# First layer's sums by a plain copy, factor and bias on GpSimd, a tanh put off near a group's end, and a scale in a register

## The chip, the cores and the metric

The kernel runs on one core of one Trainium2 chip. The metric is the device time of one execution in microseconds. A profile is one further execution, taken by the hardware profiler; its times are those of that execution alone.

A core has five engines that work side by side, each in the order of its own instruction stream: PE (TensorE, matrix products, which read SBUF and write PSUM), DVE (VectorE), ACT (ScalarE, functions of single elements), POOL (GpSimd) and SP (SyncE, which here only issues DMAs). An instruction that needs another engine's result waits for a semaphore, and what stands behind it on its engine waits too.

## The reference

One transformer layer with both branches beside each other, for 2048 rows of 512 columns: a layer norm, then attention with 32 heads of 16, and a dense network with 1792 hidden columns and GELU. Both results are added to the input. Cut to what is computed:

```python
xn = _layernorm(x, axis=-1)
# A: attention
qkv = (xn @ wqkv).reshape(B, S, 3, H, Dh).transpose(2, 0, 3, 1, 4)
scores = jnp.einsum("bhqd,bhkd->bhqk", q, k) * (Dh ** -0.5)
o = jnp.einsum("bhqk,bhkd->bhqd", _softmax(scores, axis=-1), v)
a = o.transpose(0, 2, 1, 3).reshape(B, S, D) @ wo
# B: dense network
h = jax.nn.gelu(xn @ w1 + b1, approximate=True)
b = h @ w2 + b2
return x + a + b
```

All inputs and outputs are float32.

## The kernel before

**Attention sets the beat.** Heads are taken four at a time, 8 groups, and queries 512 at a time, so there are 32 tiles (t), and each has 16 units of 128 rows. A unit (function unit) makes for one step of the schedule four score products S (128 queries by 512 keys, s_half), whose row maximum DVE takes at L259 (mt); four transposed score products T (128 keys by 512 queries, e_half), which ACT turns into exp at L304 (pe); and the products V of such exps with the values (v_half). S runs 20 units ahead of T (LEAD). Every product on PE is written as four matmuls of 32 columns each (tiled, L169), and a head's product uses half of PE's rows.

**The dense work is laid between.** In each unit PE also gets a few products D of the work that is not attention (function dense, a class Group for a sum of such products in one PSUM bank): with the pace MEAN, 3 or 4 products on each half of the rows in a unit. From about 318 to 1430 us of the profile the groups are those of the dense network, made by the function mlp. A **hidden group** makes 128 hidden columns for 512 rows: 12 products on each half, so four units. A **sum group** makes 128 rows of the second layer out of 7 hidden columns' tiles: 21 products on each half, so six units. There are 56 hidden groups and 32 sum groups.

**What follows a group.** When the last product of a group is written, the group's finish is called at once (end), and then the unit's clock goes on by one (tick). For a hidden group this is the function hidden: ACT reads the bank at L1005, multiplies by a factor and adds the bias, each a column with one value per partition, into the tile hh in SBUF. One unit later gelu starts on GpSimd: the square (L983), a scalar step (L984) and a product (L985) make the argument in the tile t (t1 in the code); then ACT takes the tanh at L972, and GpSimd makes from it and hh the two half-precision tiles g (L977 to L980), which the sum groups read as weights of their products. For a sum group the finish is store: ACT reads the bank at L1031 with the factor gs, one column too, into yt, and GpSimd adds it to the tile xa.

**Order.** The order on every engine is that in which the Python code emits. later(n, fn) calls a function n units later. pooled puts steps for GpSimd in a list with an estimate in ns for each; in every unit run_steps takes steps until 2500 ns are used up. The tanh was asked for two units behind the emission of L985, which in a row of hidden groups falls on the unit in which the next hidden group ends.

**Banks.** PSUM has eight banks. S uses three, V one, and T and D share four: T goes round three of them, and D holds one for the length of a group (hold). When a group ends, its bank goes to the end of T's round and the new group takes T's oldest. So the second T product behind a group's end is the last that finds a bank at rest; the third takes the bank that the eviction hh or yt has to empty, and the fourth the bank that the first exp behind the eviction empties.

The scale of the exps is held in a register of ACT (scale_reg), loaded once for every two groups of heads by reg_load (a TENSOR_LOAD in the trace).

Of the kernel before, what the change touches and what calls it, by code (L numbers as in the profile page):

```python
# [10 lines left out]
I32 = mybir.dt.int32  # L11
AF = mybir.ActivationFunctionType
ALU = mybir.AluOpType
# [34 lines left out]
def layer_kernel(ctx: ExitStack, tc: tile.TileContext, x, wqkv, wo, w1, b1, w2, b2, out):  # L48
    nc = tc.nc
# [45 lines left out]
    sexp = const.tile([P, 4], F32, name="sexp")  # L95
# [11 lines left out]
    def banks(tag):  # L107
        k = free_banks[tag].pop(0)
        free_banks[tag].append(k)
        return bank_tile(k, tag)  # L110
# [48 lines left out]
    def given(engine, ns):  # L159
        backlog[engine] += ns  # L160
# [37 lines left out]
            product(user, dst[j:j + 32], lhs[:, j:j + 32], rhs, start=start, stop=stop)  # L198


    scale_reg, held = nc.scalar.alloc_register("exp_scale"), [None]

    def exp_scale(m):

        if held[0] != m:
            nc.scalar.reg_load(scale_reg, sexp[0:1, m:m + 1].bitcast(I32))
            held[0] = m
        return scale_reg

    mt_of, ptiles, pv_of = {}, {}, {}  # L210
    queue, slot = [], [0]
# [1 line left out]
    def later(n, fn, local=False):  # L213
        queue.append((slot[0] + n, fn, local))
# [10 lines left out]
    def pooled(*todo):  # L225
        steps.extend(todo)
# [66 lines left out]
    def e_half(u, n):  # L293

        p, a = divmod(n, 2)
        t, kt = divmod(u, 16)
        g, qb = divmod(t, NQB)
        st = banks("T")
        r = slice(64 * a, 64 * a + 64)
        k0 = (kt % 4) * P  # L300
        tiled(None, st, kst[g % 2][p][kt // 4][r, k0:k0 + P], qst[g % 2][p][qb][r, :], True, True)
        pe = work.tile([P, QB], F32, name="pe", bufs=12)
        ptiles[u, n] = pe
        nc.scalar.activation(pe, st, AF.Exp, scale=exp_scale(g // 2))  # L304
        given("act", 470)

    def v_half(u, a):
# [234 lines left out]
    pos, spent, cur = [0], [False], [None]  # L542
# [103 lines left out]
    with ExitStack() as st1:  # L646
# [245 lines left out]
        gs = const.tile([P, 4], F32, name="gs")  # L892
# [69 lines left out]
    def mlp():  # L962
        m2 = st2p
        w2_s = m2.tile([P, 2, NF, D], F16, name="w2_s")
        b2_b = m2.tile([P, D], F32, name="b2_b")
        done = set()

        def gelu(hh, g, b, f):
            t1 = m2.tile([P, QB], F32, name="t1", bufs=2)

            def tanh():
                nc.scalar.activation(t1, t1, AF.Tanh, scale=GELU_C * GELU_A)  # L972
                given("act", 600)
                later(1, rest, True)

            def rest():
                pooled((690, lambda: nc.gpsimd.tensor_scalar(t1, t1, 1.0, gs[:, 1:2], op0=ALU.add, op1=ALU.mult)),  # L977
                       (1280, lambda: nc.gpsimd.tensor_tensor(t1, t1, hh, op=ALU.mult)),  # L978
                       (620, lambda: nc.gpsimd.tensor_scalar(g[:, 0, f, :], t1, 1.0, 0.0, op0=ALU.mult, op1=ALU.add)),
                       (1160, lambda: nc.gpsimd.tensor_tensor(g[:, 1, f, :], t1, g[:, 0, f, :], op=ALU.subtract)),  # L980
                       (0, lambda: done.add((b, f))))

            pooled((1040, lambda: nc.gpsimd.tensor_tensor(t1, hh, hh, op=ALU.mult)),  # L983
                   (620, lambda: nc.gpsimd.tensor_scalar(t1, t1, 1.0, 1.0 / GELU_A, op0=ALU.mult, op1=ALU.add)),  # L984
                   (1280, lambda: nc.gpsimd.tensor_tensor(t1, t1, hh, op=ALU.mult)),  # L985
                   (0, lambda: later(2, tanh, True)))


        HF = NF // 2
        gts, xas = {}, {}  # L990
        for k in range(NF):
            later(3 * k + 2, lambda k=k: nc.sync.dma_start(w2_s[:, :, k], w2_d[:, :, k]))
        later(12, lambda: nc.sync.dma_start(b2_b, b2[None, :].to_broadcast([P, D])))

        def hidden_group(s, f):
            b, k = s // 2, s % 2 * HF + f
            if f == 0:
                gts[s] = m2.tile([P, 2, HF, QB], F16, name="g", bufs=2)
            g, xb, wc = gts[s], xbs[b], wcs[b * NF + k]
            later(1, lambda: fetch_w1(b * NF + k + 2))  # L1000

            def hidden(hp):
                hh = m2.tile([P, QB], F32, name="hh", bufs=3)
                scale, bias = fac1[0][:, k // 2:k // 2 + 1], b1_s[:, k:k + 1]
                nc.scalar.activation(hh, hp, AF.Identity, bias=bias, scale=scale)  # L1005
                given("act", 700)
                later(1, lambda: gelu(hh, g, s, f), True)

            return Group([lambda c=c, i=i, j=j: (wc[:, i, c, :], xb[:, j, c, :]) for c in range(NC) for i, j in PAIRS],
                         dbank, hidden, pace=MEAN)  # L1010

        def sum_group(s, q):
            b, t, g = s // 2, s // 2 * 4 + q, gts[s]
            if s % 2 == 0:
                xas[t] = m2.tile([P, D], F32, name="xa", bufs=4)
                nc.sync.dma_start(xas[t], x[t * P:(t + 1) * P, :])
                later(3, lambda: pooled((1280, lambda: nc.gpsimd.tensor_tensor(xas[t], xas[t], b2_b, op=ALU.add))), True)
            xa = xas[t]
            if q == 3 and s % 2 == 0:
                fetch_x(b + 1)  # L1020
            if s == 2 * NQB - 1 and q == 1:

                ocs[2] = feed[0].tile([P, 2, NC, QB], F16, name="xb", bufs=1)
                when((NG - 2) * NQB + 2, lambda: read_o(ocs[2], 2, True), 2)
                for k in range(3):
                    acs[8 + k] = feed[0].tile([P, D], F32, name="ac", tag="wc", bufs=3)
                    later(3 + k, lambda k=k: read_acc(acs[8 + k], 8 + k))

            def store(yp):
                yt = m2.tile([P, D], F32, name="yt", bufs=2)  # L1030
                nc.scalar.activation(yt, yp, AF.Copy, scale=gs[:, 2:3])  # L1031
                given("act", 600)
                add = lambda: nc.gpsimd.tensor_tensor(xa, xa, yt, op=ALU.add)  # L1033
                put = lambda: nc.sync.dma_start(acc_d[t * P:(t + 1) * P, :], xa)
                later(1, lambda: pooled((1280, add), (0, lambda: later(4, put, True) if s % 2 else None)), True)

            return Group([lambda f=f, i=i, j=j: (g[:, i, f, q * P:(q + 1) * P], w2_s[:, j, s % 2 * HF + f, :])
                          for f in range(HF) for i, j in PAIRS], dbank, store, lambda n: (s, n // 3) in done, pace=MEAN)

        for f in range(HF):  # L1040
            yield hidden_group(0, f)
        for s in range(1, 2 * NQB + 1):
            for q in range(4):
                yield sum_group(s - 1, q)
                if s < 2 * NQB and q < 3:
                    for f in range(*((0, 3), (3, 5), (5, 7))[q]):
                        yield hidden_group(s, f)
# [143 lines left out]
```

## Time and profile before

| | |
|---|---|
| median of 3 runs | 1552.85 us (1550.26 to 1552.85) |
| the profiled execution | 1555.34 us, of which the span from the first to the last instruction is 1553.6 |
| PE busy | 1514.5 us, 97% |
| DVE busy | 1401.0 us, 90% |
| ACT busy | 1251.6 us, 81% |
| POOL busy | 674.6 us, 43% |
| mean granted PE clock | 0.993 |

Busy time is the union of an engine's instructions. PE's matmuls are pipelined and their ends are modelled, so a PE that looks busy can still be one that waits within its stream. A line such as "418.62 1.09 ACT L304 ACTIVATE pe<-pT ... x2 [0.24 <-PE pS L169]" is a row of the timeline: start and length in us, engine, source line, operation, tile written and tiles read, shapes, how many instructions are merged in the row, and in brackets how long the engine had been idle before and what ended that. In a row of groups the two numbers behind the bar are the busy time and the mean length of one in ns, and behind the second bar stands the idle time just before.

### The profile page before, as it was taken

Reading aid. Unit: us, or ns where it says so; the run is one execution under the profiler, and the core shown is the slowest. Engines: PE = TensorE matmul, PEld = TensorE weight load, DVE = VectorE, ACT = ScalarE, POOL = GpSimd, SP = SyncE. Lnnn points to the kernel's source line nnn. Section 1 sums busy time; section 2 is a strip of 40 time slices with the busy share of each in tenths; the row PEclk is TensorE's granted clock in tenths of the full one; section 3 lists DMA queues with packets and bytes.
Section 4 is the critical chain, followed back from the end, with each engine's and each line's share of the span. In section 5 each row is a group of like instructions: output and inputs, shape, how many; then the busy total and the mean of one; then the engine's idle time right before and its main releaser. Section 6 shows DMA issues by size and latency. Waiting matters only on the chain.

```text
span 1553.6 us, 86338 instructions
## 1 busy us (share of the span) xinstructions
PE 1514.5 (97%) x39203; PEld 806.0 (52%) x39203; DVE 1401.0 (90%) x2372; ACT 1251.6 (81%) x2326; POOL 674.6 (43%) x694
## 2 busy tenths in 40 slices
PE   8998999999999999999999999999999999999997
PEld 4434545555555555555555555555555555555443
DVE  7898989999999999999999999999999999999612
ACT  4316878889888888888888888888888888888771
POOL 3113697546465444435443443555254454521000
PEclk9999999999999999999999999999999999999997
DMA  6454576542111311121112111121112111022412
GB/s 210 124 158 142 167 231 197 180 120 88 50 35 47 91 33 34 36 75 42 35 56 65 46 35 35 35 80 55 36 42 60 45 35 35 22 66 60 150 50 86
DMA packets 113671, 123.72 MB, mean 80 GB/s; under 512 B 24988, under 2 KB 85276, under 8 KB 113304
## 3 DMA queue, kind: packets, MB, share of 16 engines
q1 hardware_dynamic: 113304, 118.21, 25.4%
q8 instruction: 306, 5.01, 1.4%
q14 instruction: 61, 0.50, 0.1%
HBM read 80.61 MB, written 37.34 MB: 76 GB/s over the span
## 4 chain that ended last, share of the span: by engine, by line
PE 84%; DVE 8%; ACT 2%; issue 2%; DMA 2%; SPq 1%; POOL 0%; ACTq 0%; POOLq 0%
PE pV L169 25%; PE pS L169 19%; PE pD L169 19%; PE pT L169 17%; DVE mt L259 6%; PE pT L439 1%; PE pS L439 1%; ACT pe L304 1%; ACT t L972 1%; DVE amx L667 1%; PE pT L532 1%; PE pD L439 1%; DMA ac<-acc_d 0%; PE pV L532 0%; SPq L1064 0%
## 5 line engine op out<-in xcount | busy, mean ns | idle before, releaser
L259 DVE TENSOR_REDUCE mt<-pS 128x1 f32<-128x512 f32 x2048 | 1299.9, 684 | 60.7 <-PE pS L169 43.1
L304 ACT ACTIVATE pe<-pT 128x512 f32<-128x512 f32 x2048 | 1100.0, 598 | 169.5 <-PE pS L169 72.3
L169 PE MATMUL pV<-pe,vv 64*32 64x512 f32 x8192 | 1077.6, 595 | 0.2
L169 PE MATMUL pT<-qst,kst 64*32 64x512 f16 x8192 | 708.2, 378 | 10.4 <-ACT pe L304 8.9
L169 PE MATMUL pS<-kst,qst 62*32 62x512 f16 x8192 | 636.8, 378 | 9.3 <-DVE mt L259 6.0
L169 PEld LDWEIGHTS <-qst 62*32 62x32 f16 x8192 | 271.1, 92 | 226.8 <-issue 77.9
L169 PEld LDWEIGHTS <-kst 64*32 64x32 f16 x8192 | 270.2, 91 | 213.7 <-issue 109.5
L169 PE MATMUL pD<-xb,wc 64*32 64x512 f16 x5376 | 370.5, 377 | 0.0
L169 PE MATMUL pD<-w_s,g 64*32 64x512 f16 x5376 | 359.4, 377 | 0.0
L169 PEld LDWEIGHTS pV<-pe,vv 64*32 64x32 f32 x8192 | 181.5, 105 | 111.2 <-PE pV L169 18.0
L983 POOL TENSOR_TENSOR t<-hh 128x512 f32<-128x512 f32 x56 | 58.3, 1042 | 341.2 <-ACT hh L1005 341.2
L169 PEld LDWEIGHTS <-g 64*32 64x32 f16 x5376 | 113.8, 92 | 38.6
L169 PE MATMUL pD<-xt,wqk_h 64*32 64x512 f16 x1920 | 127.6, 377 | 3.5 <-issue 3.5
L169 PEld LDWEIGHTS <-wc 64*32 64x32 f16 x5376 | 112.6, 91 | 31.1
L360 POOL TENSOR_TENSOR osb<-osb,rb 128x512 f32<-128x512 f32 x31 | 39.9, 1287 | 128.1 <-DMA rb<-den_d 95.1
L1033 POOL TENSOR_TENSOR xa<-xa,yt 128x512 f32<-128x512 f32 x32 | 41.0, 1280 | 119.0 <-ACT yt L1031 119.0
L1070 DVE SCALAR_TENSOR_TENSOR ac<-pS,gs,ac 128x512 f32<-128x512 f32 x20 | 15.0, 751 | 67.0 <-PE pT L169 46.9
L978 POOL TENSOR_TENSOR t<-t,hh 128x512 f32<-128x512 f32 x56 | 71.8, 1283 | 4.7
L985 POOL TENSOR_TENSOR t<-t,hh 128x512 f32<-128x512 f32 x56 | 71.7, 1280 | 4.7
L980 POOL TENSOR_TENSOR g<-t,g 128x512 f16<-128x512 f32 x56 | 65.3, 1166 | 4.7
L977 POOL TENSOR_SCALAR t<-t,gs 128x512 f32<-128x512 f32 x56 | 38.8, 693 | 55.5 <-ACT t L972 55.5
L169 PE MATMUL pS<-wo_s,oc 64*32 64x512 f16 x1008 | 61.7, 378 | 0.3
(139 smaller groups left out, 881.1 us busy)
## 6 DMA issues: line engine op xcount, KB each, us to landing
wch<-in_B_w_dram SPq DMA_DIRECT2D x28, 512.0 KB
wc<-w_d SPq DMA_DIRECT2D x56, 256.0 KB
qk_d<-stg SPq DMA_DIRECT2D x32, 256.0 KB
rb<-den_d SPq DMA_DIRECT2D x124, 64.0 KB
w_d<-wsp SPq DMA_DIRECT2D x28, 256.0 KB
kst<-qk_d SPq DMA_DIRECT2D x128, 48.0 KB
qst<-qk_d SPq DMA_DIRECT2D x128, 48.0 KB
xs<-in_A_x_dram SPq DMA_DIRECT2D x16, 256.0 KB
```

Source lines behind the costliest of these rows:

```text
L169: p = nc.tensor.matmul(*args, **kw)
L259: nc.vector.reduce_max(mt_of[t][:, n, qt, kb:kb + 1], s, axis=AX.X)
L304: nc.scalar.activation(pe, st, AF.Exp, scale=exp_scale(g // 2))
L360: pooled((1280, lambda: nc.gpsimd.tensor_tensor(osb, osb, rb, op=ALU.mult)), (620, lambda: nc.gpsimd.tensor_scalar(ot[:, 0], osb, 1.0, 0.0 ...
L439: nc.tensor.matmul(self.bank, lhs, rhs, start=start, stop=self.last and self.over())
L532: nc.tensor.matmul(pj, xt[:, i, c, t * P:(t + 1) * P], wh[j][:, c, :], start=(n == 0), stop=(n == 11))
L977: pooled((690, lambda: nc.gpsimd.tensor_scalar(t1, t1, 1.0, gs[:, 1:2], op0=ALU.add, op1=ALU.mult)), (1280, lambda: nc.gpsimd.tensor_tenso ...
L978: (1280, lambda: nc.gpsimd.tensor_tensor(t1, t1, hh, op=ALU.mult)),
L980: (1160, lambda: nc.gpsimd.tensor_tensor(g[:, 1, f, :], t1, g[:, 0, f, :], op=ALU.subtract)),
L983: pooled((1040, lambda: nc.gpsimd.tensor_tensor(t1, hh, hh, op=ALU.mult)), (620, lambda: nc.gpsimd.tensor_scalar(t1, t1, 1.0, 1.0 / GELU_A ...
L985: (1280, lambda: nc.gpsimd.tensor_tensor(t1, t1, hh, op=ALU.mult)),
L1033: add = lambda: nc.gpsimd.tensor_tensor(xa, xa, yt, op=ALU.add)
```

## The change

Three edits, all of them on what follows a group.

1. hidden reads the bank by a plain copy, with no factor and no bias. Both are applied by a new GpSimd instruction on hh in place, one unit later, ahead of gelu; gelu itself is called when that step has been emitted.
2. tanh asks, when its time has come, how many products the current group has left. If there is no current group (one has just ended) or no more than 8 are left on both halves together, it comes back one unit later, and is then emitted in any case.
3. store's scale is read from a register of ACT. The code for the exp's register is made general (factor takes the register and the place it is loaded from, and loads it only if it changes).

```diff
-    scale_reg, held = nc.scalar.alloc_register("exp_scale"), [None]
-
-    def exp_scale(m):
-
-        if held[0] != m:
-            nc.scalar.reg_load(scale_reg, sexp[0:1, m:m + 1].bitcast(I32))
-            held[0] = m
-        return scale_reg
+    exp_scale, sum_scale = (nc.scalar.alloc_register(n) for n in ("exp_scale", "sum_scale"))
+    held = {}
+
+    def factor(reg, src):
+
+        if held.get(reg.name) != str(src):
+            nc.scalar.reg_load(reg, src.bitcast(I32))
+            held[reg.name] = str(src)
+        return reg
...
-        nc.scalar.activation(pe, st, AF.Exp, scale=exp_scale(g // 2))
+        nc.scalar.activation(pe, st, AF.Exp, scale=factor(exp_scale, sexp[0:1, g // 2:g // 2 + 1]))
...
-            def tanh():
+            def tanh(again=1):
+                if again and (cur[0] is None or cur[0].left(0) + cur[0].left(1) <= 8):
+                    later(1, lambda: tanh(0), True)
+                    return
                 nc.scalar.activation(t1, t1, AF.Tanh, scale=GELU_C * GELU_A)
...
-                nc.scalar.activation(hh, hp, AF.Identity, bias=bias, scale=scale)
-                given("act", 700)
-                later(1, lambda: gelu(hh, g, s, f), True)
+                nc.scalar.activation(hh, hp, AF.Copy)
+                given("act", 600)
+                later(1, lambda: pooled((690, lambda: nc.gpsimd.tensor_scalar(hh, hh, scale, bias, op0=ALU.mult, op1=ALU.add)),
+                                        (0, lambda: gelu(hh, g, s, f))), True)
...
-                nc.scalar.activation(yt, yp, AF.Copy, scale=gs[:, 2:3])
+                nc.scalar.activation(yt, yp, AF.Copy, scale=factor(sum_scale, gs[0:1, 2:3]))
```

What this does to the order: PE's and DVE's streams are the same, instruction for instruction. On ACT, here is the order before from the end of the third hidden group to the tanh behind the fifth (L304 is the exp, L330 the copy of an attention tile's result; the numbers behind t tell one tile from another):

```order
L1005 ACTIVATE hh<-pD,b_s,fac_2410 128x512
L972 ACTIVATE t_8536<-t_8536 128x512
L304 ACTIVATE pe<-pT 128x512 x16
L1005 ACTIVATE hh<-pD,b_s,fac_2410 128x512
L972 ACTIVATE t_8906<-t_8906 128x512
L304 ACTIVATE pe<-pT 128x512 x16
L1005 ACTIVATE hh<-pD,b_s,fac_2410 128x512
L304 ACTIVATE pe<-pT 128x512 x2
L330 ACTIVATE osb<-pV 128x512
L304 ACTIVATE pe<-pT 128x512 x2
L972 ACTIVATE t_9280<-t_9280 128x512
```

And the same place after the change, where the lines are L1009 for hh, L976 for the tanh, L305 for the exp and L331 for osb:

```order
L1009 ACTIVATE hh<-pD 128x512
L305 ACTIVATE pe<-pT 128x512 x4
L976 ACTIVATE t_8538<-t_8538 128x512
L305 ACTIVATE pe<-pT 128x512 x12
L1009 ACTIVATE hh<-pD 128x512
L305 ACTIVATE pe<-pT 128x512 x4
L976 ACTIVATE t_8909<-t_8909 128x512
L305 ACTIVATE pe<-pT 128x512 x12
L1009 ACTIVATE hh<-pD 128x512
L305 ACTIVATE pe<-pT 128x512 x2
L331 ACTIVATE osb<-pV 128x512
L305 ACTIVATE pe<-pT 128x512 x14
```

The tanh of the group before has moved from right behind hh to behind the four exps that follow it. Before, 27 of the 56 tanhs stand right behind an hh; after, one does. 18 tanhs still stand 16 exps behind their own hh, 31 stand 20 behind, and 7 stand 28 or 32 behind.

On GpSimd, the steps from the second hidden group's square to the third's before the change:

```order
L983 TENSOR_TENSOR t_8536<-hh 128x512
L984 TENSOR_SCALAR t_8536<-t_8536 128x512
L985 TENSOR_TENSOR t_8536<-t_8536,hh 128x512
L977 TENSOR_SCALAR t_8171<-t_8171,gs 128x512
L978 TENSOR_TENSOR t_8171<-t_8171,hh 128x512
L979 TENSOR_SCALAR g<-t_8171 128x512
L980 TENSOR_TENSOR g<-t_8171,g 128x512
L983 TENSOR_TENSOR t_8906<-hh 128x512
```

and after it, where the square is L987 and the new instruction L1011:

```order
L1011 TENSOR_SCALAR hh<-hh,fac_2410,b_s 128x512
L987 TENSOR_TENSOR t_8538<-hh 128x512
L988 TENSOR_SCALAR t_8538<-t_8538 128x512
L989 TENSOR_TENSOR t_8538<-t_8538,hh 128x512
L981 TENSOR_SCALAR t_8172<-t_8172,gs 128x512
L982 TENSOR_TENSOR t_8172<-t_8172,hh 128x512
L983 TENSOR_SCALAR g<-t_8172 128x512
L984 TENSOR_TENSOR g<-t_8172,g 128x512
L1011 TENSOR_SCALAR hh<-hh,fac_2410,b_s 128x512
L987 TENSOR_TENSOR t_8909<-hh 128x512
```

One step with two columns as operands is new ahead of each square; the rest keeps its order here. On SP four groups of DMAs change places with their neighbours, none of them by more than five rows.

## The prediction

> **What bounds the kernel now.** I read the page first (span, chain of waits), then the stretch in which the changed lines run, then ScalarE's timeline there, cycle by cycle.
>
> ```profile
> span 1553.6 us, 86338 instructions
> PE 84%; DVE 8%; ACT 2%; issue 2%; DMA 2%; SPq 1%; POOL 0%; ACTq 0%; POOLq 0%
> 318.00:1430.00 1112.00, 1102.73 (x30748) 603.24 (x30742) 1071.50 (x1768) 983.98 (x1834) 514.68 (x518) 1.00 0.18 50
> L304 ACT ACTIVATE pe<-pT 128x512 f32<-128x512 f32 x1664 | 893.1, 598 | 120.5 <-PE pS L169 58.6 <-PE pT L169 37.2
> L1005 ACT ACTIVATE hh<-pD,b_s,fac 128x512 f32<-128x512 f32 x56 | 43.6, 778 | 3.9
> L972 ACT ACTIVATE t<-t 128x512 f32<-128x512 f32 x56 | 35.4, 631 | 0.0
> L1031 ACT ACTIVATE yt<-pD,gs 128x512 f32<-128x512 f32 x32 | 22.0, 689 | 3.6 <-PE pT L169 0.3 <-PE pS L169 0.2
> L330 ACT ACTIVATE osb<-pV 128x512 f32<-128x512 f32 x26 | 15.8, 606 | 0.0
> ```
>
> The third line is the view of the stretch from 318 to 1430 us, the whole life of the changed lines: busy time of PE, PE's weight loads, VectorE, ScalarE, GpSimd, then PE's granted clock (full). The others are groups of that stretch: line, engine, tiles, shape, count, busy us, mean ns, idle time before. The chain names PE, and PE looks 99% busy, VectorE 96%, ScalarE 88%, GpSimd 46%. By these shares ScalarE has 128 us to spare and none of the three edits should matter. But PE is in order, and a matmul that waits for a PSUM bank holds up all behind it. So I look for places where ScalarE is late for a moment.
>
> ```profile
> 413.38 2.24 ACT L304 ACTIVATE pe<-pT 128x512 f32<-128x512 f32 x4 [0.28 <-PE pS L169]
> 415.66 0.78 ACT L1005 ACTIVATE hh<-pD,b_s,fac 128x512 f32<-128x512 f32 x1
> 416.34 2.05 ACT L304 ACTIVATE pe<-pT 128x512 f32<-128x512 f32 x4
> 418.62 1.09 ACT L304 ACTIVATE pe<-pT 128x512 f32<-128x512 f32 x2 [0.24 <-PE pS L169]
> 419.87 1.08 ACT L304 ACTIVATE pe<-pT 128x512 f32<-128x512 f32 x2 [0.16 <-PE pS L169]
> 421.26 2.30 ACT L304 ACTIVATE pe<-pT 128x512 f32<-128x512 f32 x4 [0.30 <-PE pT L169]
> 423.83 2.24 ACT L304 ACTIVATE pe<-pT 128x512 f32<-128x512 f32 x4 [0.28 <-PE pS L169]
> 426.18 0.78 ACT L1005 ACTIVATE hh<-pD,b_s,fac 128x512 f32<-128x512 f32 x1
> 426.86 0.62 ACT L972 ACTIVATE t<-t 128x512 f32<-128x512 f32 x1
> 427.37 2.05 ACT L304 ACTIVATE pe<-pT 128x512 f32<-128x512 f32 x4
> ...
> 434.87 2.24 ACT L304 ACTIVATE pe<-pT 128x512 f32<-128x512 f32 x4 [0.28 <-PE pS L169]
> ```
>
> This is ScalarE's timeline over two hidden groups of four units each (start, us, count, idle time before). They are alike except that the second has a tanh right behind hh. From 413.38 to 423.83 the first takes 10.45 us, from 423.83 to 434.87 the second 11.04: **0.59 us more, the whole of the tanh**, although ScalarE idles about 1 us in each cycle (0.28, 0.24, 0.16, 0.30). The idle time lies elsewhere, before the other exps. PE's timeline says why.
>
> ```profile
> 416.40 0.40 PE L169 MATMUL pS<-kst,qst 62*32 62x512 f16 x4
> 416.49 0.40 PE L169 MATMUL pT<-qst,kst 64*32 64x512 f16 x4
> 416.70 0.40 PE L169 MATMUL pS<-kst,qst 62*32 62x512 f16 x4
> 416.97 0.40 PE L169 MATMUL pT<-qst,kst 64*32 64x512 f16 x4
> ```
>
> ```profile
> 427.22 0.40 PE L169 MATMUL pS<-kst,qst 62*32 62x512 f16 x4
> 428.01 0.40 PE L169 MATMUL pT<-qst,kst 64*32 64x512 f16 x4 [0.39 <-ACT pe L304]
> ```
>
> These are the third and fourth pT behind a group's end (only the fourth in the second fence). The third needs the bank that hh empties: it starts at 416.49, and hh ends at 415.66 + 0.78 = 416.44. The fourth needs the bank of the first exp after hh. With the tanh ahead, that exp starts at 427.37 and is over 0.59 later, at 427.96; pT starts at 428.01, 0.79 behind the pS before it, where 0.21 is PE's own step (416.49 to 416.70). Without the tanh: exp over at 416.93, pT at 416.97, 0.27 behind its pS. PE waits in both, little in the one and 0.58 in the other.
>
> **The change, part by part.** PE's and VectorE's instructions stand in the same order before and after. What changes is ScalarE's order, 56 instructions more on GpSimd, and four small swaps on SP.
>
> *Tanh put off.* Of 27 tanhs that stand right behind an hh, 26 move behind the next four exps. What is gained at most is 0.59 each. What it costs at the new place:
>
> ```profile
> 315.95 2.24 ACT L304 ACTIVATE pe<-pT 128x512 f32<-128x512 f32 x4 [0.28 <-PE pS L169]
> ...
> 326.62 2.24 ACT L304 ACTIVATE pe<-pT 128x512 f32<-128x512 f32 x4 [0.28 <-PE pS L169]
> ```
>
> ```profile
> 359.60 2.24 ACT L304 ACTIVATE pe<-pT 128x512 f32<-128x512 f32 x4 [0.28 <-PE pS L169]
> ...
> 365.01 0.67 ACT L972 ACTIVATE t<-t 128x512 f32<-128x512 f32 x1
> ...
> 370.48 2.24 ACT L304 ACTIVATE pe<-pT 128x512 f32<-128x512 f32 x4 [0.28 <-PE pS L169]
> ```
>
> The trace has such cycles: the first has hh, two exps and the copy osb, with no tanh, 10.67 us; the second has in addition a tanh four exps behind hh, just where the change puts it, 10.88 us. There it costs 0.21, with osb already filling ScalarE's idle time. None of the 26 has an osb ahead of it. Then, from the first cycle above, ScalarE idles 0.24 before 418.62; a tanh takes 0.51 (426.86 to 427.37), so the next exps come 0.27 late, 0.10 if hh is 0.17 shorter, and the idle 0.16 and 0.30 behind take that up before a bank is short. So the cost is between 0 and 0.21; I take 0.06, near the cycle without osb. Gain 26 x (0.59 - 0.06) = **13.8 us**; at the ends 15.3 and 9.9.
>
> *hh as a plain copy.* It goes from 778 ns to what the same kind of copy from PSUM takes, osb's 606: 0.17 less. The first exp behind hh then ends at 416.76 in place of 416.93, and pT could start at 416.80. But the pS at 416.40 doesn't move, the pT behind it comes at about 416.41, its pS one step of 0.21 later at 416.62, the fourth pT at 416.83: PE gains 0.14, and is then its own bound. 56 x 0.14 = **7.8 us**, bounds 0 (another wait follows) and 56 x 0.17 = 9.5. After the tanh's move this wait is the one that is left at a group's end, and 0.14 of it goes; what is late next is PE's own step.
>
> *yt with its scale in a register.* 689 becomes 606: 32 x 0.083 = 2.7 at most, 0 at least. It holds a bank as hh does, but PE has more products left there; I take 0.06 each, near the upper end: **1.9 us**.
>
> ```profile
> L206 ACTq TENSOR_LOAD <-sexp x4: 274/278/674, 126.9 to 1172.4; - x4
> L977 POOL TENSOR_SCALAR t<-t,gs 128x512 f32<-128x512 f32 x56 | 38.8, 693 | 55.5 <-ACT t L972 55.5
> L984 POOL TENSOR_SCALAR t<-t 128x512 f32<-128x512 f32 x56 | 34.8, 621 | 4.9
> 418.35 1.27 POOL L985 TENSOR_TENSOR t<-t,hh 128x512 f32<-128x512 f32 x1
> ```
>
> *What is added.* One register load, by the first row 0.3 us of ScalarE's sequencer (a first one 0.67). One group end now has a tanh behind hh and another four exps later: 0.2. Together **-0.5**. GpSimd gets 56 instructions with two column operands. With none such a one takes 621, with one 693, so with two about 765 to 790 ns, some 44 us on an engine that idles 597 us of the stretch. The new wait is GpSimd's: its square waits for the affine step, the tanh for the square, and behind the tanh on ScalarE stand the exps. In the cycle above the last product ahead of the tanh ends at 419.62 and the tanh starts at 426.86: 7.2 us of slack, from which about 0.9 goes and to which a put-off tanh adds a unit. So I cost it at nothing; with the cover gone, each us that GpSimd is late would be a us of ScalarE, 56 times. On SP one store of ot passes a dn load and four K loads, and three other DMAs swap with neighbours; what they carry is used units later. Nothing.
>
> **Sum:** 13.8 + 7.8 + 1.9 - 0.5 = 23.0 us. The profiled execution took 1555.34 (span 1553.6 and 1.7 around it): 1532.3 for it. It stands 2.5 above the median of the runs shown, 1552.85; the same sum from there gives **1529.9**. Bounds: 15.3 + 9.5 + 2.7 - 0.5 = 27.0, so 1525.9; and 9.9 - 0.5 = 9.4, so 1543.5.
>
> **Rivals.**
> *1. Only the wait is spread.* The tanh costs its 0.21 everywhere, and the shorter hh and yt gain nothing, as another engine's wait follows at once: 1543.5. For it: the cycle with osb, and PE at 99%. Against: the fourth pT at 416.97 starts 0.04 behind the exp that it waits for.
> *2. ScalarE's total counts, not the place.* If it stays behind through the whole group, the move gains nothing and only the shorter evictions do: 9.5 + 2.7 - 0.5 = 11.7, so 1541.2. Against: 0.24, 0.16 and 0.30 of idle time in the same cycle.
> *3. GpSimd holds up VectorE, and it gets slower.* The place is the reduction mt, 1768 times in the stretch.
>
> ```profile
> L259 DVE TENSOR_REDUCE mt<-pS 128x1 f32<-128x512 f32 x12 | 7.7, 686 | 0.4 <-PE pS L169 0.4
> L259 DVE TENSOR_REDUCE mt<-pS 128x1 f32<-128x512 f32 x15 | 9.5, 684 | 0.9 <-PE pS L169 0.8
> ```
>
> The price would be the 44 us of new GpSimd time, if VectorE stood still for it: 1552.85 - 23.0 + 44 = 1574. It decides against the change from 23.0 / 1768 = 13 ns on each reduction. Against: these are VectorE's reductions in two stretches, first 408.2 to 415.6 us, where GpSimd does nothing, then 427.1 to 437.3, where it is busy nearly throughout: 686 and 684 ns each. The Trainium skill ("SBUF — State Buffer", section Terms) speaks for this rival: VectorE and GpSimd share a pair of ports, and whoever loses it stands still until the other's instruction is over. By that rule the sum would be this rival's; by the two rows the reductions, which read PSUM, don't feel it, and I go by the rows.
> *4. It doesn't do what it says*: hh takes the time it took, and the tanh's stall comes back a unit later: 1552.85, no change.
>
> **How the numbers follow.** Forecast 0.66, rival 1 0.14, rival 2 0.11, rival 3 0.04, rival 4 0.05. The range goes from 1524 (upper bound of the gain, and the runs' own spread) to 1544, which takes in rivals 1 and 2. About 0.2% (3 us) is what a measurement of this kernel can tell from no change: faster 0.91, same 0.05, slower 0.04.
>
> **What would show it.** On ScalarE's timeline hh at 0.60, four exps, then the tanh, and the cycles of four units at 10.3 to 10.4 us, with tanh and without. On PE no pT behind a group's end that starts 0.05 behind an exp's end. If the cycle with a tanh stays 0.2 longer than the one without, the term of 13.8 was too big; if the one without stays at 10.45, the 7.8 was wrong. Reductions longer than 690 ns, or ScalarE idle before a tanh with GpSimd as the releaser, would make the sign wrong.

## The result and the profile after

| | before | after |
|---|---|---|
| median | 1552.85 us (1550.26 to 1554.21, 4 runs) | **1530.31 us** (1529.35 to 1531.15, 4 runs) |
| the profiled execution | 1555.34, span 1553.6 | 1530.44, span 1528.7 |

The ratio is 0.9857, with a 95% interval of 0.984 to 0.9874: 1.4% faster. The prediction was 1529.9 us, in a range of 1524 to 1544.

The chain of waits on the page of the changed kernel, and the stretch of the dense network, first before and then after (length, then busy time of PE, PE's weight loads, VectorE, ScalarE, GpSimd, then the granted clock). Both rows are cut at the same work: from the exps ahead of the first hidden group's end to the exps behind the last sum group's end.

```profile
PE 88%; DVE 8%; issue 1%; DMA 1%; ACT 1%; SPq 0%; POOL 0%; ACTq 0%; POOLq 0%
```

```profile
315.95:1426.61 1110.66, 1101.39 (x30712) 602.34 (x30696) 1070.17 (x1765) 982.72 (x1831) 513.39 (x517) 1.00 0.18 50
316.01:1402.86 1086.85, 1085.26 (x30712) 614.05 (x30696) 1067.97 (x1765) 968.58 (x1831) 556.70 (x573) 1.00 0.18 52
```

The stretch is 23.8 us shorter at the same clock. PE looks as busy as before (99.9% of the stretch, before 99.2%), so its share hardly shows what went. VectorE's row does: its 1765 instructions take nearly the same time (1070.2 and 1068.0 us), and its idle time falls from 40.5 to 18.9 us. The groups of ScalarE and GpSimd from 318 to 1404 us show the edits (count, busy us, mean ns):

```profile
L1009 ACT ACTIVATE hh<-pD 128x512 f32<-128x512 f32 x56 | 33.4, 597 | 3.6
L1036 ACT ACTIVATE yt<-pD 128x512 f32<-128x512 f32 x32 | 19.1, 597 | 3.7 <-PE pT L169 0.4 <-PE pS L169 0.2
```

```profile
L1011 POOL TENSOR_SCALAR hh<-hh,fac,b_s 128x512 f32<-128x512 f32 x56 | 43.3, 772 | 287.1 <-ACT hh L1009 287.1
```

hh went from 778 to 597 ns (so rival 4, that it takes the time it took, falls), yt from 689 to 597, and GpSimd's new step takes 772 ns, 43.3 us in all. ScalarE's timeline over the same two hidden groups that the prediction read:

```profile
410.18 2.24 ACT L305 ACTIVATE pe<-pT 128x512 f32<-128x512 f32 x4 [0.28 <-PE pS L169]
412.46 0.60 ACT L1009 ACTIVATE hh<-pD 128x512 f32<-128x512 f32 x1
412.95 2.06 ACT L305 ACTIVATE pe<-pT 128x512 f32<-128x512 f32 x4
...
420.45 2.24 ACT L305 ACTIVATE pe<-pT 128x512 f32<-128x512 f32 x4 [0.28 <-PE pS L169]
422.80 0.60 ACT L1009 ACTIVATE hh<-pD 128x512 f32<-128x512 f32 x1
423.29 2.06 ACT L305 ACTIVATE pe<-pT 128x512 f32<-128x512 f32 x4
425.20 0.66 ACT L976 ACTIVATE t<-t 128x512 f32<-128x512 f32 x1
...
430.79 2.24 ACT L305 ACTIVATE pe<-pT 128x512 f32<-128x512 f32 x4 [0.28 <-PE pS L169]
```

The cycle without a tanh takes 420.45 - 410.18 = 10.27 us (before 10.45), the one with a tanh 430.79 - 420.45 = 10.34 (before 11.04). The tanh stands four exps behind hh, and 0.07 of its 0.59 is left. PE's timeline at the first of these ends, the third and the fourth transposed score product (pT) with the score products beside them:

```profile
413.20 0.40 PE L169 MATMUL pS<-kst,qst 62*32 62x512 f16 x4
413.27 0.40 PE L169 MATMUL pT<-qst,kst 64*32 64x512 f16 x4
413.49 0.40 PE L169 MATMUL pS<-kst,qst 62*32 62x512 f16 x4
413.60 0.40 PE L169 MATMUL pT<-qst,kst 64*32 64x512 f16 x4
```

hh ends at 412.46 + 0.60 = 413.06, well ahead of the third. The first exp behind hh ends at 412.95 + 0.60 = 413.55, and the fourth pT starts 0.05 later: **it still waits for ScalarE**, though less (0.11 behind its pS, where it was 0.27).

Cutting both traces at the first exp of each unit in which a group ends gives 87 cycles, which have the same work before and after. "Turn" stands for cycles at whose start a tile's row maxima are turned (explained with the experiments).

| cycles | count | gain in all, us | each | by the prediction's terms |
|---|---|---|---|---|
| hidden, a tanh stood right behind hh | 20 | 13.7 | 0.69 | 0.53 + 0.14 |
| the same, with a turn | 7 | 3.3 | 0.47 | 0.53 + 0.14 |
| hidden, no tanh behind hh | 25 | 5.5 | 0.22 | 0.14 |
| the same, with a turn | 4 | 0.0 | 0.00 | 0.14 |
| sum groups | 28 | 1.2 | 0.04 | 0.06 |
| the same, with a turn | 3 | 0.0 | 0.01 | 0.06 |

One of the 20 keeps a tanh behind hh and gained 0.18. In four places the cut between two cycles hides something: before the change a tanh stood just ahead of the first exp of a sum group's cycle and put that exp off, as at 451.39 on ScalarE's timeline before:

```profile
450.87 0.65 ACT L972 ACTIVATE t<-t 128x512 f32<-128x512 f32 x1
451.39 2.09 ACT L304 ACTIVATE pe<-pT 128x512 f32<-128x512 f32 x4
```

After the change this tanh lies four exps behind yt, in the sum group's cycle. So 0.26 of the gain of four hidden cycles with a turn (0.53 to 0.60 each) is this tanh's, and their first four units gain 0.27 to 0.34, as the other three with a turn do (0.34). The four sum groups' cycles look 0.16 longer for the same reason (their first four units take 10.25 before, 10.41 after); without a tanh such a cycle takes 10.51 before and 10.42 after, so the tanh costs nothing where it lies now.

In all, the cycles gain 23.7 us of the 24.9 by which the span got shorter. The other 1.1 lies behind the stretch, where nothing was changed; it is less than the runs of one kernel differ by.

### The profile page after: what moved, and what is told of

The parts are those of the page before. It is cut to its first block, busy times and chain, and to the rows that moved or that the text cites. A ratio compares the mean times of both kernels' runs of the same rounds, so it can differ in the third digit from the quotient of the medians.

```text
span 1528.7 us, 86384 instructions
## 1 busy us (share of the span) xinstructions
PE 1499.2 (98%) x39203; PEld 818.1 (54%) x39203; DVE 1398.8 (92%) x2372; ACT 1237.3 (81%) x2326; POOL 717.9 (47%) x750
## 4 chain that ended last, share of the span: by engine, by line
PE 88%; DVE 8%; issue 1%; DMA 1%; ACT 1%; SPq 0%; POOL 0%; ACTq 0%; POOLq 0%
PE pV L169 26%; PE pD L169 20%; PE pS L169 20%; PE pT L169 17%; DVE mt L260 6%; PE pT L440 1%; PE pS L440 1%; DVE amx L668 1%; PE pT L533 1%; PE pD L440 1%; PE pV L533 0%; DMA wq<-in_A_wqkv_dram 0%; SPq L404 0%; DVE ac L1075 0%; PE pT L738 0%
## 5 line engine op out<-in xcount | busy, mean ns | idle before, releaser
L305 ACT ACTIVATE pe<-pT 128x512 f32<-128x512 f32 x2048 | 1102.8, 600 | 159.3 <-PE pT L169 69.5
L169 PE MATMUL pS<-kst,qst 62*32 62x512 f16 x8192 | 629.3, 378 | 7.8 <-DVE mt L260 5.7
L169 PEld LDWEIGHTS <-qst 62*32 62x32 f16 x8192 | 277.6, 92 | 231.6 <-issue 76.2
L169 PEld LDWEIGHTS <-kst 64*32 64x32 f16 x8192 | 273.8, 91 | 168.9 <-issue 57.9
L1011 POOL TENSOR_SCALAR hh<-hh,fac,b_s 128x512 f32<-128x512 f32 x56 | 43.3, 772 | 287.1 <-ACT hh L1009 287.1
L987 POOL TENSOR_TENSOR t<-hh 128x512 f32<-128x512 f32 x56 | 58.3, 1042 | 4.1
```

What stands on the lines that cost most here:

```text
L169: p = nc.tensor.matmul(*args, **kw)
L305: nc.scalar.activation(pe, st, AF.Exp, scale=factor(exp_scale, sexp[0:1, g // 2:g // 2 + 1]))
L1011: later(1, lambda: pooled((690, lambda: nc.gpsimd.tensor_scalar(hh, hh, scale, bias, op0=ALU.mult, op1=ALU.add)), (0, lambda: gelu(hh, g, ...
```

## The experiments

Times are medians, with the ratio to the kernel before in runs of the same chip, and its 95% interval. Cycle times are read from the one profile of each kernel. Two profiles of the changed kernel agree within 0.03 us in 85 of the 87 cycles, but two sum groups' cycles, those at 519.91 and 1367.92 us, differ by 1.13 and 0.50. What these two show is not put down to an edit.

### Each edit alone

`tanh_alone` is the kernel before with edit 2 only:

```diff
-            def tanh():
+            def tanh(again=1):
+                if again and (cur[0] is None or cur[0].left(0) + cur[0].left(1) <= 8):
+                    later(1, lambda: tanh(0), True)
+                    return
```

> Only the tanh is put off; hh keeps its 778 ns with factor and bias on ScalarE, yt its 689. Stall theory (the forecast's): 27 tanhs leave the group's end, 0.59 each less 0.06 to 0.21 at the new place, which may be nearer the upper end since hh is still long: 10 to 14 us, so 1539 to 1543; cycles with a tanh at 10.5 to 10.65 us, those without stay at 10.45. Rival 1 (wait only spread): the lower end, 1543. Rival 2 (ScalarE's total counts, not the place): no change, 1552.85, cycles with a tanh stay at 11.04.

Measured: 1543.92 us, ratio 0.9936 (0.9918 to 0.9953). ScalarE's timeline over the same two groups:

```profile
411.82 2.24 ACT L304 ACTIVATE pe<-pT 128x512 f32<-128x512 f32 x4 [0.28 <-PE pS L169]
...
422.27 2.24 ACT L304 ACTIVATE pe<-pT 128x512 f32<-128x512 f32 x4 [0.28 <-PE pS L169]
424.62 0.78 ACT L1008 ACTIVATE hh<-pD,b_s,fac 128x512 f32<-128x512 f32 x1
425.30 2.05 ACT L304 ACTIVATE pe<-pT 128x512 f32<-128x512 f32 x4
427.20 0.66 ACT L975 ACTIVATE t<-t 128x512 f32<-128x512 f32 x1
...
432.79 0.60 ACT L304 ACTIVATE pe<-pT 128x512 f32<-128x512 f32 x1 [0.28 <-PE pS L169]
```

With hh still 0.78 long, the first cycle stays at 10.45, and the second falls from 11.04 to 10.52: the same work on ScalarE, 0.52 less time. Rival 2 (ScalarE's total counts, not the place) falls here.

Over all hidden groups the cycles gain 13.8 us, the figure of the prediction's term, but not all of it comes from the 27 tanhs that stood behind an hh. They gained 12.6: 20 of them 0.52 each, and the seven in cycles with a turn 0.27 to 0.34. Another 1.0 comes from the four tanhs that left the unit ahead of a sum group's cycle, and 0.2 from one cycle that is 0.28 shorter in `register_alone` too.

And the time gains less, since 4.0 us are lost in sum groups, 0.9 of it in one of the two cycles that differ between profiles of one kernel. The other 3.1 are the same four tanhs: each was due one unit ahead of a group's end with 8 or fewer products left, and the rule put it off **onto** the end, right behind yt. Each of these cycles grew by 0.77, to 11.02 where a sum group's cycle without a tanh takes 10.51, so 0.51 is what the place costs.

`copy_alone` is the kernel before with edit 1 only, so the tanh comes when it is due. As the new GpSimd step starts gelu later, 22 tanhs stand right behind an hh, where 27 did.

```diff
-                nc.scalar.activation(hh, hp, AF.Identity, bias=bias, scale=scale)
-                given("act", 700)
-                later(1, lambda: gelu(hh, g, s, f), True)
+                nc.scalar.activation(hh, hp, AF.Copy)
+                given("act", 600)
+                later(1, lambda: pooled((690, lambda: nc.gpsimd.tensor_scalar(hh, hh, scale, bias, op0=ALU.mult, op1=ALU.add)),
+                                        (0, lambda: gelu(hh, g, s, f))), True)
```

> Only hh becomes a plain copy, with factor and bias on GpSimd; the tanh comes when it is due, as before, which puts 22 of them right behind an hh (27 before, since GpSimd's steps shift the plan). Stall theory: 56 x 0.14 to 0.17 = 7.8 to 9.5 us and some 2 to 3 us for the five tanhs: 10 to 12 us, so 1541 to 1543; cycles without a tanh at 10.28 to 10.31 us, those with one right behind hh at 10.86 to 10.90. Rival 1: only the five tanhs, 1550. Rival 2: 9.5, 1543, and the cycles with a tanh no longer than without by more than ScalarE's idle time leaves.

Measured: 1540.58 us, ratio 0.9925 (0.9896 to 0.9953). The same view:

```profile
407.90 2.24 ACT L304 ACTIVATE pe<-pT 128x512 f32<-128x512 f32 x4 [0.28 <-PE pS L169]
...
418.17 2.24 ACT L304 ACTIVATE pe<-pT 128x512 f32<-128x512 f32 x4 [0.28 <-PE pS L169]
420.51 0.60 ACT L1005 ACTIVATE hh<-pD 128x512 f32<-128x512 f32 x1
421.00 0.62 ACT L972 ACTIVATE t<-t 128x512 f32<-128x512 f32 x1
...
429.02 0.60 ACT L304 ACTIVATE pe<-pT 128x512 f32<-128x512 f32 x1 [0.28 <-PE pS L169]
```

10.27 without the tanh, 10.85 with it. The shorter hh gains its full 0.18 in both, and the tanh's 0.58 is back. So the two edits act on the same wait and add up: neither hides the other, and rival 1 (a shorter hh gains nothing) falls.

`register_alone` is the kernel before with edit 3 only:

```diff
-                nc.scalar.activation(yt, yp, AF.Copy, scale=gs[:, 2:3])
+                nc.scalar.activation(yt, yp, AF.Copy, scale=factor(sum_scale, gs[0:1, 2:3]))
```

> Only yt's scale is in a register. Stall theory: 32 x 0.06 to 0.083 = 1.9 to 2.7 us less 0.3 for the load, 1550.5 to 1551.3, and the cycles that begin with yt 0.06 to 0.09 us shorter (10.51 before). Rival 1: no change at all, cycles at 10.51.

Measured: 1551.72 us, ratio 0.9977 (0.9963 to 0.9991). A cycle that begins with a sum group's end, where the kernel before takes 10.51 (its timeline has the exps at 590.07 and 600.58):

```profile
591.38 2.32 ACT L305 ACTIVATE pe<-pT 128x512 f32<-128x512 f32 x4 [0.28 <-PE pS L169]
...
601.80 0.60 ACT L305 ACTIVATE pe<-pT 128x512 f32<-128x512 f32 x1 [0.28 <-PE pS L169]
```

10.42, so yt's whole 0.09 counts. In the stretch the three parts gain 9.8, 13.3 and 2.7 us, 25.8 together, where the change gains 23.8. The copy alone already moves five tanhs away from the end, which the tanh's rule would move as well.

### GpSimd with more work

`pool_more` is the changed kernel with two more steps on GpSimd behind the new one, which multiply hh by 1 and add 0:

```diff
+                                        (0, lambda: nc.gpsimd.tensor_scalar(hh, hh, 1.0, 0.0, op0=ALU.mult, op1=ALU.add)),
+                                        (0, lambda: nc.gpsimd.tensor_scalar(hh, hh, 1.0, 0.0, op0=ALU.mult, op1=ALU.add)),
                                         (0, lambda: gelu(hh, g, s, f))), True)
```

> The changed kernel with two more instructions on GpSimd behind each affine step (times one, plus zero, on hh in place): 112 x 0.62 = 69 us more of GpSimd, with ScalarE's, PE's and VectorE's streams as in the changed kernel. Stall theory: GpSimd's time is covered, as the smallest slack ahead of a tanh in the changed kernel is 4.4 us: 1530 within 2 us, reductions at 683 to 686 ns. Rival 3 (GpSimd holds up VectorE through a shared port): up to 69 us longer, reductions longer by up to 30 ns; if the 43 us of the affine steps already cost something, at least 10 us longer.

Measured: 1533.51 us, ratio 0.9867 (0.9837 to 0.9898), which can't be told from the change by the time. The group of one of the two steps on GpSimd (the other's reads alike), the group of VectorE's reductions, and PE's timeline at the one place that got over 0.3 us longer:

```profile
L1013 POOL TENSOR_SCALAR hh<-hh 128x512 f32<-128x512 f32 x56 | 34.8, 621 | 4.6
```

```profile
L260 DVE TENSOR_REDUCE mt<-pS 128x1 f32<-128x512 f32 x1657 | 1050.2, 684 | 18.5 <-PE pS L169 5.8
```

```profile
399.73 0.40 PE L169 MATMUL pD<-w_s,g 64*32 64x512 f16 x4 [0.62 <-POOL g L984]
```

GpSimd has 69.6 us more, and VectorE's reductions take 684 ns on average, where the changed kernel has 683. Rival 3 (GpSimd holds up VectorE) falls: with its price it would have cost all of that. What GpSimd does cost is 2.2 us in one cycle, which takes 12.57 in place of 10.38: it holds the end of the first sum group, whose last products wait for the last hidden tile's g, in the row above for the last step of it. The stretch is 2.3 us longer than in the change. The last g ends at 399.67, 2.45 us behind the first exp of that unit (397.22); in the changed kernel it ends 0.11 ahead of it (398.53 + 1.16 = 399.69, against 399.80). So this is the one place where these runs show the cover to be thin.

### What is left of the wait

`eighth_read` is the changed kernel with an hh of 64 columns read in place of 512 (GpSimd spreads them over the tile), so ScalarE's eviction takes 0.22 us; seven eighths of the hidden sums are left out. It is run beside `after_again`, the changed kernel itself.

```diff
-                nc.scalar.activation(hh, hp, AF.Copy)
+                hx = m2.tile([P, 64], F32, name="hx", bufs=1)
+                nc.scalar.activation(hx, hp[:, 0:64], AF.Copy)
...
-                later(1, lambda: pooled((690, lambda: nc.gpsimd.tensor_scalar(hh, hh, scale, bias, op0=ALU.mult, op1=ALU.add)),
+                later(1, lambda: pooled((690, lambda: nc.gpsimd.tensor_scalar(hh.rearrange("p (a n) -> p a n", a=8), hx.unsqueeze(1).to_broadcast([P, 8, 64]), scale, bias, op0=ALU.mult, op1=ALU.add)),
```

> The changed kernel with hh's read of the bank cut to 64 of 512 columns (the other seven eighths of the hidden sums are left out; GpSimd spreads the 64 over hh, so all else is as long as before). ScalarE's read goes from 0.60 to about 0.23 us. If PE is its own bound at a group's end once hh takes 0.60, as the forecast has it: no change, cycles at 10.27. If ScalarE still sets the cycle: up to 0.3 us less for each of the 56, as much as 16 us.

> The changed kernel once more, as the measure for the three beside it on the same chip: about 0.986 of the kernel before, cycles without a tile's turn at 10.27 us with a tanh and without, nine cycles with a turn at 10.70.

Measured: `eighth_read` 1524.84 us, ratio 0.9809 (0.9783 to 0.9835); `after_again` 1533.02, 0.9865 (0.9842 to 0.9888). ScalarE's timeline of `eighth_read` at the same end, PE's row of the third and fourth pT, and the engines' busy time in this cycle (length, PE, weight loads, VectorE, ScalarE, GpSimd) in the kernel before, in the changed kernel and in `eighth_read`:

```profile
407.70 2.24 ACT L305 ACTIVATE pe<-pT 128x512 f32<-128x512 f32 x4 [0.28 <-PE pS L169]
409.98 0.22 ACT L1010 ACTIVATE hx<-pD 128x64 f32<-128x64 f32 x1
410.22 2.15 ACT L305 ACTIVATE pe<-pT 128x512 f32<-128x512 f32 x4
...
417.83 2.24 ACT L305 ACTIVATE pe<-pT 128x512 f32<-128x512 f32 x4 [0.28 <-PE pS L169]
```

```profile
410.80 0.59 PE L169 MATMUL pT<-qst,kst 64*32 64x512 f16 x8
```

```profile
413.38:423.83 10.45, 10.45 (x300) 5.60 (x288) 10.14 (x17) 9.24 (x17) 2.94 (x3) 1.00 0.20 54
410.18:420.45 10.27, 10.27 (x300) 5.95 (x288) 10.14 (x17) 9.07 (x17) 3.72 (x4) 1.00 0.20 57
407.70:417.83 10.13, 10.13 (x300) 5.68 (x288) 10.09 (x17) 8.89 (x17) 3.71 (x4) 1.00 0.19 58
```

The cycle takes 10.13: of 0.38 us less on ScalarE, 0.14 still count. The two products now stand in one row, the fourth at about 410.99 (a product of four matmuls takes 0.40, two take 0.59), and the exp that it needs was over at 410.82. That is 3.29 behind the cycle's start, where the change has 413.60 - 410.18 = 3.42. Only here does the fourth pT start clearly behind its exp, by 0.17. So the change left 0.14 of ScalarE's lateness at a regular hidden end (0.20 where the cycle holds a tanh), 7.0 us over all hidden groups. The cycles with a turn stayed at 10.70.

What sets the 10.13 isn't shown. PE's own pace is one candidate, VectorE is the other: its 17 instructions take 10.09 to 10.14 us in all three rows, so of its idle time of 0.31 in the kernel before only 0.04 is left. With so little left there, a still shorter read on ScalarE could hardly shorten this cycle further.

### The cycles that don't move

Nine cycles of four units take 10.70 us in the changed kernel whatever else they hold. Six of them took 10.70 before and gained nothing, three took 11.04. Five longer cycles begin with the same four units, and these take 10.69 or 10.70 too. Once a tile the row maxima are negated, turned by small products on PE and converted to two half-precision parts on VectorE (mhl), and in these fourteen that falls at a group's end. First VectorE's first conversion there in the changed kernel (the second takes 0.22), then ScalarE's in it and in `eighth_read`:

```profile
684.35 0.20 DVE L281 TENSOR_SCALAR mhl<-pS 64x64 f16<-64x64 f32 x1
```

```profile
681.92 2.24 ACT L305 ACTIVATE pe<-pT 128x512 f32<-128x512 f32 x4 [0.28 <-PE pS L169]
...
686.06 1.09 ACT L305 ACTIVATE pe<-pT 128x512 f32<-128x512 f32 x2 [0.29 <-PE pT L169]
...
692.61 0.60 ACT L305 ACTIVATE pe<-pT 128x512 f32<-128x512 f32 x1 [0.28 <-PE pS L169]
```

```profile
678.49 2.24 ACT L305 ACTIVATE pe<-pT 128x512 f32<-128x512 f32 x4 [0.28 <-PE pS L169]
...
682.64 1.09 ACT L305 ACTIVATE pe<-pT 128x512 f32<-128x512 f32 x2 [0.43 <-PE pT L169]
...
689.19 1.09 ACT L305 ACTIVATE pe<-pT 128x512 f32<-128x512 f32 x2 [0.28 <-PE pS L169]
```

692.61 - 681.92 = 10.69, and 689.19 - 678.49 = 10.70. ScalarE just idles longer ahead of the same exp (0.43 in place of 0.29), so it isn't what holds these. Five kernels changed the turn, each from the changed kernel.

`turn_on_act` makes the first conversion on ScalarE, and `turn_both_act` both of them:

```diff
-            nc.vector.tensor_scalar_mul(mhl[:, 0], pt[:64, :64], 1.0 / MROW)
-            nc.vector.scalar_tensor_tensor(mhl[:, 1], pt[:64, :64], 1.0 / MROW, mhl[:, 0], op0=ALU.mult, op1=ALU.subtract)
+            nc.scalar.activation(mhl[:, 0], pt[:64, :64], AF.Copy, scale=1.0 / MROW)
+            nc.scalar.activation(mhl[:, 1], pt[:64, :64], AF.Copy, scale=1.0 / MROW)
```

> The changed kernel with the first of VectorE's two conversions at a tile's turn (mhl, 0.22 us, 32 times) as a ScalarE copy. If VectorE's extra work at a turn sets the cycles of 10.70 us that did not get shorter: up to 0.2 us less for each turn, some 5 us. If it is PE's wait for the turned rows or its four small products: no change. Against it: ScalarE now waits in order for PE there, which can cost 0.2 us and more a turn.

> As the one beside it, with both conversions on ScalarE and the second without its subtraction (the low half of the row maxima is left out, as a probe). If VectorE sets the turn: 0.43 us less of it, cycles with a turn up to 0.4 us shorter, some 10 us; if it is PE: no change or slower.

Measured: `turn_on_act` 1533.47 us, 0.9878 (0.9853 to 0.9902), the nine cycles at 10.55 to 11.09; `turn_both_act` 1532.25, 0.9862 (0.984 to 0.9884), eight of them at 10.70 and one at 10.98. VectorE is busy for 10.59 of the 10.69 us of the cycle at 681.92 in the changed kernel, which makes it look like the bound; but in `turn_both_act` it idles for 0.35 of the same cycle, which still takes 10.70. VectorE's conversions don't set them.

`turn_t_bank` gives the turned maxima a bank of T's round in place of one of S's three, `turn_one` makes one product of 128 rows and one store in place of two each, and `turn_one_t` does both:

```diff
-            pt = banks("S")
+            pt = banks("T")
...
-                nc.tensor.matmul(pt[32 * a:32 * a + 32, :64], mneg[64 * a:64 * a + 64, :],
-                                 ident[64 * a:64 * a + 64, 64 * a:64 * a + 64], start=True, stop=True)
+            nc.tensor.matmul(pt[:32, :P], mneg, ident, start=True, stop=True)
```

> The changed kernel with the turned maxima of a tile written to a bank of T's round in place of one of S's three. If the cycles of 10.70 us are set by score products that wait for an S bank, which VectorE's reductions empty one after another: cycles with a turn 0.2 to 0.4 us shorter, 3 to 8 us in all, unless T's round, one bank short there, gives it back. If they are set by the four small products themselves on PE: no change at 10.70.

> The changed kernel with one product of 128 rows in place of the two of 64 that turn a tile's maxima, one store in place of two, and the two conversions on 32 rows of 128. If PE's small products set the 10.70: up to 0.3 us less for each turn. If the S bank does: no change, or 0.1 us longer, as the conversions grow.

> Both together. If both the bank and the small products count, the shortest cycles with a turn of the three; if only the bank does, as with the bank of T's round alone.

Measured: 1531.12 us, 0.9856 (0.9836 to 0.9875), the nine cycles at 10.65 to 10.80; 1531.47, 0.9851 (0.9835 to 0.9868), 10.76 to 10.84; 1532.71, 0.9861 (0.9844 to 0.9879), 10.75 to 10.84. None gains more than 0.05 in one of these cycles. **What sets the 10.70 stays open**: it isn't ScalarE's eviction, VectorE's two conversions, the choice of the bank or the count of products, each taken alone. Whether two of these are near enough that one replaces the other wasn't tried, but for the one pair in `turn_one_t`.

### The same move for another instruction

`osb_late` is the changed kernel with the copy osb of an attention tile's result put behind four exps of its unit in place of two:

```diff
-        nc.scalar.activation(osb, pv, AF.Copy)
-        given("act", 600)
-        free_banks["S"].append(k)
+
+        def read(k=k):
+            nc.scalar.activation(osb, pv, AF.Copy)
+            given("act", 600)
+            free_banks["S"].append(k)
+
+        later(0, read, True)
```

> The changed kernel with the copy osb of an attention tile's result put behind four exps of its unit in place of two, as the tanh was; 14 of the 32 copies come four exps behind a group's eviction in place of two, 4 of them beside a tanh. If what counts is that a bank's reader stands ahead of the fourth T product's exp, the ten without a tanh gain 0.17 to 0.2 us a cycle (10.44 to 10.50 becomes 10.27 to 10.34 behind hh, 10.59 becomes 10.42 behind yt): 1.7 to 2 us, too little for the clock, to be read from the cycles; those with a tanh gain nothing. If ScalarE's total counts: no cycle changes. Against it: the bank of the result comes free half a unit later.

Measured: 1533.0 us, ratio 0.9863 (0.9841 to 0.9886). ScalarE's timeline of one such cycle in the changed kernel, then in `osb_late`:

```profile
316.01 2.24 ACT L305 ACTIVATE pe<-pT 128x512 f32<-128x512 f32 x4 [0.28 <-PE pS L169]
...
319.79 0.62 ACT L331 ACTIVATE osb<-pV 128x512 f32<-128x512 f32 x1
...
326.50 0.60 ACT L305 ACTIVATE pe<-pT 128x512 f32<-128x512 f32 x1 [0.28 <-PE pS L169]
```

```profile
313.29 2.24 ACT L305 ACTIVATE pe<-pT 128x512 f32<-128x512 f32 x4 [0.28 <-PE pS L169]
...
318.03 0.64 ACT L333 ACTIVATE osb<-pV 128x512 f32<-128x512 f32 x1
...
323.80 0.60 ACT L305 ACTIVATE pe<-pT 128x512 f32<-128x512 f32 x1 [0.28 <-PE pS L169]
```

10.49 and 10.51: no gain. Of the other 25 cycles with an osb twelve stay as they were, ten are 0.04 to 0.19 longer than in the changed kernel, two are 0.46 and 0.98 longer (the latter is one of the two that differ between profiles of one kernel), and one is 0.20 shorter, behind a cycle that is 0.27 longer. Behind seven of the twelve the next cycle is 0.18 to 0.32 longer, where osb now stands just ahead of the cut. In all, the cycles of `osb_late` lose 3.8 us, 1.0 of it in that one doubtful cycle. osb was already behind the first exp that follows hh, the one that the fourth pT needs. Its cost of about 0.22 over a cycle without it (10.27) is therefore another wait. osb empties the bank of the V products, while a tanh of the same length at the same place, which empties none, costs 0.00 to 0.07; that the bank is the reason is argued from this, not shown.

## Why the prediction was right, and where it was not

*The stall and its mechanism.* Right. PE's view named the fourth pT behind a group's end and the exp that it waits for, and the cycles followed that one wait: 0.52 from the move alone, 0.18 from the copy alone, 0.70 (11.04 to 10.34) from both.

*The tanh's term, 13.8.* The mechanism held, the size in part by luck. The 27 tanhs behind an hh gained 12.6 in `tanh_alone`; the 13.8 that its hidden cycles show has 1.0 of other tanhs in it and 0.2 of a cycle that got shorter without this edit too. The cost at the new place, taken as 0.06, was 0.00 to 0.07 in regular cycles (10.27 or 10.34 against 10.27). What was not foreseen is the turn: with one a cycle stops at 10.70, so seven of the moves gained 0.27 to 0.34 in place of 0.67 in the change, 2.4 us less together. The trace before showed it: six cycles without a tanh behind the group's end stood at 10.70, where the prediction took one cycle of 10.45 and one of 11.04 as the measure for all. Not foreseen either was that the rule moves tanhs that did not stand behind an hh. It put four of them across the end of a sum group, which cost 0.51 each in `tanh_alone` and nothing in the change, where they came four exps later.

*The copy's term, 7.8.* The sum came out near, but one step of it failed: "PE gains 0.14, and is then its own bound". It set PE's own step from the pS to the fourth pT at 0.21, so that pT could not start before 3.45 us of the cycle. It started at 3.42, 0.11 behind its pS, still 0.05 behind the exp's end, which the prediction itself had named as a sign that should be gone: the gain was 0.18, the whole of what the eviction got shorter by, and `eighth_read`, where pT starts at 3.29, shows that another 0.14 was to be had. The 0.21 was read between a pT and the pS behind it (416.49 to 416.70), and was used for the step from that pS to the next pT as well. The reading that the third pT waits for hh hardly holds either: with hh over at 2.88 us of the cycle in place of 3.06, that pT came at 3.09 in place of 3.11. Against `tanh_alone`, the change gains 0.00 or 0.01 in each of the eleven hidden cycles with a turn, where 0.14 was forecast, and 0.18 in most of the 45 others, 8.7 us in all.

*yt's term, 1.9.* A little more than forecast. Of the 31 cycles, leaving out the two that differ between profiles of one kernel, yt's 0.09 counted in 22, 1.9 us, and also in the four that a tanh moved into (10.42 without one, 10.41 with it). The three with a turn didn't change. `register_alone` has 2.4 us over all 31.

*What was costed at nothing.* Right in the cycles read here. The row of GpSimd's last product ahead of a tanh in the changed kernel:

```profile
415.86 1.29 POOL L989 TENSOR_TENSOR t<-t,hh 128x512 f32<-128x512 f32 x1
```

It ends at 417.15, and the tanh that needs it starts at 425.20, 8.1 us later (7.2 before): the slack grew, since the tanh was put off by more than the 0.77 that GpSimd took. The new step was put at 765 to 790 ns and took 772. The register load, costed at 0.3, took 0.28 on ScalarE's sequencer, but the cycle in which it stands gained its 0.08 by yt like the others.

*Rival 3 and the Trainium skill.* The reductions took 683 ns with 43 us more on GpSimd, and 684 with another 70. The sentence of the Trainium skill that spoke for this rival ("SBUF — State Buffer", section Terms) has the loser of the shared ports stand still, and names no condition. The same page of the Trainium skill, in its section "SBUF: two separate sides", limits this to VectorE's instructions in a two-port mode or with two inputs in SBUF. The reductions have one input, in PSUM, and their times agree with the narrower wording; in which mode they ran no run here shows.

The total was as near as it was (23.0 forecast, 23.7 in the cycles) partly by luck, because errors of both signs met: the eleven hidden cycles with a turn gained 3.0 us less than the terms gave them, and the 45 others 2.9 more, yt 0.3 more, and the 0.5 set aside for what was added did not show.

## What to carry to other kernels

An engine at 99% busy can still hold waits in its own stream: look for two cycles that differ by one instruction of another engine, and see whether the time between them is the whole of that instruction. List every kind of cycle before multiplying: here 11 of 56 hidden cycles had another limit, which stood in the trace before. What counts then is the place in the other engine's stream and not its total, and the place is narrow: here only what stands ahead of the first exp behind a group's end. A rule that puts work off must look at where it lands, not only at where it leaves, as four tanhs in `tanh_alone` showed that were put off onto the end. And where cycles are cut at an instruction that can itself be late, a gain in one and a loss in the next can be one and the same delay on either side of the cut.

## What the runs showed of the hardware

ScalarE's copy of a 128x512 tile from PSUM takes 597 ns with its scale in a register, as with no scale at all, 689 with one column as operand and 778 with two: each column costs about 90 ns. On GpSimd a step of the same size takes 621, 693 to 697 and 772 ns with none, one and two columns, about 75 each.

The time that PE's waits cost is hardly to be seen in its idle time. The groups of pT, before from 318 to 1430 us and after from 318 to 1404 (idle time behind the last bar):

```profile
L169 PE MATMUL pT<-qst,kst 64*32 64x512 f16 x6652 | 574.3, 378 | 7.8 <-ACT pe L304 7.8
```

```profile
L169 PE MATMUL pT<-qst,kst 64*32 64x512 f16 x6640 | 567.0, 377 | 0.3 <-ACT pe L305 0.3
```

7.5 us of idle time went, and the stretch got 23.8 us shorter; VectorE's idle time fell by 21.6. PE's rows overlap (above, the pS of 413.20 and the pT of 413.27 run side by side), so a wait of some tenths of a us within its stream seldom leaves it idle.
